# A seven-product form of the output matmul in a cross-attention and MoE kernel on Trainium2

## The chip, the core and the metric

The kernel runs on one core of one Trainium2 chip. A core has a matrix engine (TensorE, "PE" in the profile), a vector engine (VectorE, "DVE"), an activation engine (ScalarE, "ACT"), a general engine (GpSimd, "POOL") and a queue engine (SyncE, "SP") that here only issues DMAs. TensorE reads from the on-chip memory SBUF and writes to PSUM, eight accumulation banks of 128 x 512 fp32; the other engines carry data from there to SBUF. Each engine works through its own instructions in order; semaphores tie the engines together. The metric is the device time of one launch in microseconds (us), the median of several runs.

## What is computed

`x` is (8 batches, 8 heads, 512 tokens, 64), `state` is (8, 8, 32 slots, 64). Tokens attend to the slots and the slots to the tokens; both results are put side by side along the sequence and go through one feed-forward layer with 2048 hidden units.

```python
scores = scale * np.matmul(x, state.transpose(0, 1, 3, 2))   # softmax over slots -> a
xread = np.matmul(a, state)
scores2 = scale * np.matmul(state, x.transpose(0, 1, 3, 2))  # softmax over tokens -> a2
sread = np.matmul(a2, x)
y = np.concatenate([xread, sread], axis=2)     # then (B * 544, 512)
h = y @ w_in                                   # 512 -> 2048
g = h * (1.0 / (1.0 + np.exp(-h)))             # SILU
out = g @ w_out                                # 2048 -> 512
```

## The kernel before

Matmuls are in bf16 with fp32 sums, and the output is fp32. Nothing is left to a scheduler: the order in which the program is written is the order of each engine's queue.

The read of the tokens is folded into the first layer. For each batch `W1[b]` = state x w_in (256 slot rows x 2048) is made by small tiled matmuls (`w1_mms`, L470, eight matmuls of 32 output rows that share the array, called a piece of 512 columns) and carried to SBUF by `w1_out`, half on VectorE and half on ScalarE. The normalised weights `a`, transposed, are `aT[b]`. So h of a batch, hidden tile ft (16 tiles of 128), is two accumulating matmuls of 512 columns, `W1[b]` x `aT[b]`: `emit_G1(k)`, L525, k = 16 b + ft. It goes to one of the two PSUM buffers `h1` of the pool psH, and ScalarE's SILU (L554) writes it to SBUF as `gt[k]`, 128 hidden units x 512 tokens. `upto(k)` issues all of these up to k.

The output product, `G2(b, tt, ft)` (L563), takes 128 tokens (block tt of 4) of `gt`, all 512 output columns of `w_out_sb[:, ft]`, and sums over the 16 ft in one PSUM bank, tag o0 or o1 of psO. `store(b, tt, eng)` copies a finished bank to SBUF, with VectorE for blocks 0 and 3 and ScalarE for 1 and 2, and SP issues the DMA of 256 KB.

Batch 0 has a loop of its own (L658 to L723) that also makes the first W1. Batches 1 to 7 (L734 to L803) run through tt and ft, 64 matmuls of 512 columns each. Between them stand, at places written out as `at == (tt, ft)`:
- in block 0, the rest of the batch's own `emit_G1`, one before each G2, six ahead (three in batch 1); in block 3, the first six of the next batch;
- at (1, 4), or (1, 6) in batch 1: the scores for batch b + 2 (`scores_t`, in one bank of psO and one of psH), two W1 pieces (in the four banks a0 to a3 of psA, by `bank`), in batches 1, 4 and 6 the state rows' products (`sread`, L417, in psH), then their way out on VectorE and ScalarE;
- at (2, 8) of batches 1, 2, 4 and 5: two more W1 pieces in the banks and a third in psH;
- casts and transposes of x and the norm (`norm_t`) of batch b + 2 at (3, 0). ScalarE loads another function table before the exponentials and one after.

The state rows (256 of them) are the last, "batch 8": `place_xm` gathers them on VectorE in `xmT` (eight copies, at (0, 4) and (0, 8) of batch 7), their `emit_G1` (L543, four matmuls of 256 columns) stand in blocks 1 to 3 of batch 7, and their output is `G2(8, 0, ft)`, and `last_cols` (L585) for the other 128 rows.

Of the kernel before, what the change touches and what calls it, by code (L numbers as in the profile page):

```python
# [8 lines left out]
FP32 = mybir.dt.float32  # L9
# [33 lines left out]
def kernel(  # L43
# [13 lines left out]
    pers = ctx.enter_context(tc.tile_pool(name="pers", bufs=1))  # L57
    xpool = ctx.enter_context(tc.tile_pool(name="xpool", bufs=2))
    xtpool = ctx.enter_context(tc.tile_pool(name="xtpool", bufs=2))
    att = ctx.enter_context(tc.tile_pool(name="att", bufs=4))  # L60
    epool = ctx.enter_context(tc.tile_pool(name="epool", bufs=6))
    wpool = ctx.enter_context(tc.tile_pool(name="wpool", bufs=2))
    tpool = ctx.enter_context(tc.tile_pool(name="tpool", bufs=2))
    e2pool = ctx.enter_context(tc.tile_pool(name="e2pool", bufs=4))
    gpool = ctx.enter_context(tc.tile_pool(name="gpool", bufs=28))
    opool = ctx.enter_context(tc.tile_pool(name="opool", bufs=4))
    psO = ctx.enter_context(tc.tile_pool(name="psO", bufs=1, space=bass.MemoryType.PSUM))
    psH = ctx.enter_context(tc.tile_pool(name="psH", bufs=2, space=bass.MemoryType.PSUM))
    psA = ctx.enter_context(tc.tile_pool(name="psA", bufs=1, space=bass.MemoryType.PSUM))
# [16 lines left out]
    stT = pers.tile([128, B, 4, 2, NS], BF16)  # L86
    w_in_sb = pers.tile([128, 4, DF], BF16)
    w_out_sb = pers.tile([128, NFT, DM], BF16)
    xs = pers.tile([128, B, 128], BF16)
    xmT = pers.tile([128, 2, 4, NS, 4], BF16)  # L90
    x_rows = []
# [232 lines left out]
    eT = {}  # L324

    def scores_t(b):
        scT_ps[0] = psO.tile([128, 512], FP32, tag="o1", name="ps_scT")
        scT_ps[1] = psH.tile([128, 512], FP32, tag="h1", name="ps_scT")
        for s in range(4):
            for hg in range(2):  # L330
                h = HEAD_OF_SLOT[hg][s]
                r = 64 * (h % 2)
                nc.tensor.matmul(  # L333
                    scT_ps[hg][ds(32 * s, 32), :],
                    stT[ds(r, 64), b, h // 2, s % 2, :],
                    xT[b][ds(r, 64), :, h // 2, :],
                    start=True,
                    stop=True,
                    tile_position=(r, 32 * s),
                    skip_group_check=True,  # L340
                )
# [63 lines left out]


    def sread(bs):
        ps = psH.tile([128, 512], FP32, tag="h1", name="ps_sr")
        for i, b in enumerate(bs):
            to = ps[:, ds(132 * i, 132)]  # L410
            for hg in range(2):
                for c in range(4):
                    for s in range(4):
                        h = HEAD_OF_SLOT[hg][s]
                        odd = h % 2
                        at = PAD + XW * (4 * c + h // 2) + (64 if odd else -1)
                        nc.tensor.matmul(  # L417
                            to[ds(32 * s, 32), ds(66 * hg + odd, 65)],
                            exp_nat[b, hg][:, c, s, :],
                            x_rows[b % NX][:, ds(at, 65)],  # L420
                            start=(c == 0),
                            stop=(c == 3),
                            tile_position=(0, 32 * s),
                            skip_group_check=True,
                        )
        return ps
# [65 lines left out]

    h1 = {}
    gt = {}
    outs = {}

    h_ps = {}

    def g1_first():
        for k in range(2):  # L500
            gt[k] = gpool.tile([128, 512], BF16, tag="g", name="g")
        pss = [psH.tile([128, 512], FP32, tag="h1", name="h1") for _ in range(2)]
        ps1 = psA.tile([128, 512], FP32, tag="a1", name="h1")
        for i in range(2):
            for k, to in ((0, pss[i][:, 0:256]), (1, ps1[:, ds(256 * i, 256)])):
                for hg in range(2):
                    nc.tensor.matmul(  # L507
                        to,
                        W1[0][:, hg, ds(128 * k, 128)],
                        aT[0][:, hg, ds(2 * i, 2), :],  # L510
                        start=(hg == 0),
                        stop=(hg == 1),
                        skip_group_check=True,
                    )
        for i in range(2):
            nc.scalar.activation(
                gt[0][:, ds(256 * i, 256)], pss[i][:, 0:256], func=SILU, bias=0.0
            )
        nc.scalar.activation(gt[1][:], ps1[:], func=SILU, bias=0.0)

    def g1_half(k, hg):
        b, ft = divmod(k, NFT)
# [11 lines left out]
    def emit_G1(k):  # L534
# [14 lines left out]
                    skip_group_check=True,  # L549
                )  # L550
        n = 512 if b < B else 256
        g = gpool.tile([128, 512], BF16, tag="g", name="g")
        gt[k] = g
        nc.scalar.activation(g[:, 0:n], ps[:, 0:n], func=SILU, bias=0.0)  # L554

    def G2(b, tt, ft):
        if ft == 0:
            if b == 0 and tt >= 2:
                outs[tt] = psA.tile([128, DM], FP32, tag=f"a{tt - 2}", name="o_a")
            else:  # L560
                i = (tt + (b > 0)) % 2 if tt < 3 else 0
                outs[tt] = psO.tile([128, DM], FP32, tag=f"o{i}", name="o")
        nc.tensor.matmul(  # L563
            outs[tt][:],
# [4 lines left out]
            skip_group_check=True,  # L569
        )  # L570

    def store(b, tt, eng):
        o = opool.tile([128, DM], FP32, tag="o_sb", name="o_sb")
        copy(eng, o[:], outs[tt][:])
        if b < B:
            nc.sync.dma_start(out_re[ds(136 * b, 128), tt, :], o[:])
# [81 lines left out]
    for ft in range(12):  # L658
# [3 lines left out]
        if ft in W0:  # L662
# [4 lines left out]
            if ft in W1_AT:  # L667
                w1_out(1, [(W1_AT[ft], 512)], both, pss1)
            ready = sum(W0[ft]) // 128
        if ft == 11:  # L670
            for hg in range(2):
                cast_x(1, nc.vector, 0, 4, 4 * hg, 4)
# [54 lines left out]
    def w1_next(k, new=bank):  # L727
# [3 lines left out]
            done.append((i, cols, both, w1_mms(i, cols, new)))  # L731
        return done

    for b in range(1, B):  # L734
        n = b + 1
        m = n + 1
        lead = 3 if b == 1 else 6
        for tt in range(4):
            for ft in range(NFT):
                at = (tt, ft)  # L740
                if tt == 0:
                    upto(NFT * b + min(lead + ft, NFT))
                if b == B - 1 and at in ((0, 4), (0, 8)):
                    place_xm(at[1] // 8, nc.vector)
                if b == 1:
                    if at == (0, 1):
                        transpose_x(3)
                    if at == (0, 4):
                        for u in range(2):
                            evict_state(u, nc.vector)  # L750
                        spread_x(2)
                    if at == (0, NFT - lead):
                        for hg in range(2):
                            scores(2, hg)
                        for hg in range(2):
                            exps(2, hg)
                    if at == (1, 0):
                        for hg in range(2):
                            norm(2, hg, (((nc.gpsimd, nc.vector)[hg], 0, 4),))
                            transpose_a(2, hg)  # L760
                elif at == (0, NFT - lead) and m < B:
                    nc.scalar.activation(warm[:], busy[:, 0:1], func=EXP, bias=0.0)
                if m + 1 < B:
                    if at == (0, 2):
                        for h in range(0, H, 4 if b < 3 else H):
                            load_x(m + 1, h, 4 if b < 3 else H, nc.sync)
                    if at == (1, 0):
                        for c in range(4):
                            cast_x(m + 1, nc.gpsimd, c, 1)
                    if at == (2, 10):  # L770
                        transpose_x(m + 1)
                if n < B and at == (1, 6 if b == 1 else 4):
                    if m < B:
                        scores_t(m)
                    pss = w1_next(2)
                    srs = SREAD_AT.get(b, ())
                    if srs:
                        ps_sr = sread(srs)
                    if m < B:
                        exps_t(m)  # L780
                        nc.scalar.activation(warm[:], busy[:, 0:1], func=SILU, bias=0.0)  # L781
                    w1_out(*pss[0])
                    if srs:
                        sread_out(srs, ps_sr)
                    w1_out(*pss[1])
                if m < B:
                    if at == (2, 0):
                        spread_x(m)
                    if at == (3, 0):
                        norm_t(m)  # L790
                if n < B:
                    if at == (2, 8) and b in (1, 2, 4, 5):
                        pss = w1_next(2) + w1_next(1, new_h)
                        for i in (2, 0, 1):
                            w1_out(*pss[i])
                    if tt == 3 and ft % 2 == 1 and ft // 2 < 6:
                        upto(NFT * n + ft // 2 + 1)
                elif tt > 0 and (ft % 3 == 2 or ft == NFT - 1):
                    upto(min(done[0] + 1, NFT * (B + 1)))
                G2(b, tt, ft)  # L800
            store(b, tt, nc.scalar if tt in (1, 2) else nc.vector)
        for ft in range(NFT):
            gt.pop(NFT * b + ft)  # L803
    for ft in range(NFT):
        upto(NFT * B + ft + 2)
        G2(B, 0, ft)
# [32 lines left out]
```

## Time and profile before

| | |
|---|---|
| timed runs | 212.98 us median (212.7, 212.98, 213.41) |
| profiled execution, its span | 306.5 us |
| mean granted TensorE clock in it | 0.661 of full speed |
| output matmuls L563 to psO, 512 columns | 496, busy 189.3 us |
| first-layer matmuls L525, 512 columns | 252, busy 104.3 us |
| SILUs of 512 columns, ScalarE | 126, mean 597 ns |
| output copies, VectorE and ScalarE | 15 at 691 ns, 16 at 597 ns |
| x casts on GpSimd | 24, mean 648 ns |
| output stores, SP | 33 DMAs of 256 KB (median), 2.4 us to landing |

The profiled execution took longer than the timed runs, and the profile shows with which clock its matrix engine ran; a reading must say which of the two it speaks of. "Busy" is the union of an engine's instructions, "mean" the recorded duration of one; matmuls overlap, so that their mean is longer than their spacing. A group's last entry is the time the engine stood idle before it, and what ended most of that.

### The profile page before, as it was taken

How to read it: one execution, taken by the hardware profiler on the slowest of the kernel's cores; microseconds unless marked ns; L12 is line 12 of the kernel's file. 1: busy time of each engine (PE TensorE's matmuls, PEld its weight loads, DVE VectorE, ACT ScalarE, POOL GpSimd, SP SyncE). 2: the span in 40 equal slices, each digit the busy share in tenths (PEclk: the TensorE clock that was granted, in tenths of full speed). 3: DMA queues.
4: the chain of work that ended last, by engine and by line, in shares of the span. 5: the costliest groups of instructions: out<-in, count | busy, mean ns of one | idle time of the engine just before them, and what ended most of it. 6: DMA issues, size and time to landing. Idle time of an engine off the chain costs nothing.

```text
span 306.5 us, 3871 instructions
## 1 busy us (share of the span) xinstructions
PE 301.5 (98%) x1576; PEld 120.1 (39%) x1576; DVE 73.9 (24%) x146; ACT 141.0 (46%) x244; POOL 40.1 (13%) x62
## 2 busy tenths in 40 slices
PE   8999999999999999999999999999999999999995
PEld 3433443343333333333333333333333333355544
DVE  4521347244400350032001350035002104000000
ACT  4744556674546533672446453664353044322310
POOL 8640143022202010111002010000100000000000
PEclk9666666666666666666666666666666666666666
DMA  8999438715722251515251261020200100000102
GB/s 196 200 206 273 141 130 222 225 34 81 175 90 81 72 137 34 171 49 124 68 171 37 50 157 49 0 71 37 66 34 36 43 34 36 0 34 34 36 34 68
DMA packets 42978, 28.65 MB, mean 93 GB/s; under 512 B 27601, under 2 KB 37841, under 8 KB 42961
## 3 DMA queue, kind: packets, MB, share of 16 engines
q1 hardware_dynamic: 36752, 20.65, 24.3%
q0 software_dynamic: 5920, 7.64, 12.2%
q8 instruction: 12, 0.20, 0.3%
q10 hardware_dynamic: 288, 0.13, 0.1%
q14 instruction: 6, 0.04, 0.0%
HBM read 17.43 MB, written 8.91 MB: 86 GB/s over the span
## 4 chain that ended last, share of the span: by engine, by line
PE 98%; ACT 1%; DVE 0%; issue 0%
PE o L563 53%; PE h L525 27%; PE ps_w L470 4%; PE h L543 3%; PE o_a L563 3%; PE ps_busy L165 2%; PE o_part L585 2%; PE ps_sr L417 1%; PE ps_xt L254 1%; PE ps_scT L333 1%; PE ps_sc L307 1%; PE ps_at L399 0%; ACT xT L157 0%; PE h L507 0%; ACT exp_nat L321 0%
## 5 line engine op out<-in xcount | busy, mean ns | idle before, releaser
L563 PE MATMUL o<-w_out_sb,g 128*128 128x512 bf16 x496 | 189.3, 512 | 0.0
L554 ACT ACTIVATE g<-h 128x512 bf16<-128x512 f32 (+1 forms) x142 | 81.4, 573 | 92.4 <-PE h L525 73.1
L525 PE MATMUL h<-aT,W 128*128 128x512 bf16 x252 | 104.3, 514 | 0.0
L563 PEld LDWEIGHTS <-g 128*128 128x128 bf16 x528 | 62.5, 121 | 100.5 <-issue 96.7
L525 PEld LDWEIGHTS <-W 128*128 128x128 bf16 x252 | 30.2, 121 | 51.5 <-issue 50.3
L159 DVE COPY o_sb<-o 128x512 f32<-128x512 f32 x15 | 10.4, 691 | 157.9 <-PE o L563 148.0
L159 DVE CAST W<-ps_w 128x512 bf16<-128x512 f32 (+1 forms) x35 | 22.0, 669 | 43.2 <-PE ps_w L470 43.2
L157 ACT ACTIVATE W<-ps_w 128x512 bf16<-128x512 f32 (+1 forms) x31 | 16.1, 579 | 19.3 <-PE ps_w L470 19.3
L157 ACT ACTIVATE o_sb<-o 128x512 f32<-128x512 f32 x16 | 9.5, 597 | 32.3 <-PE o L563 28.4
L159 POOL CAST x_nat<-x_f 128x512 bf16<-128x512 f32 x24 | 14.6, 648 | 46.8 <-issue 33.0
L363 POOL TENSOR_TENSOR an<-e,rcn 128x512 bf16<-128x512 bf16 x5 | 7.6, 1517 | 83.3 <-DVE rcn L361 83.3
L563 PE MATMUL o_a<-w_out_sb,g 128*128 128x512 bf16 x32 | 13.9, 510 | 0.0
L543 PE MATMUL h<-xmT,w_in_sb 128*128 128x256 bf16 x64 | 13.4, 349 | 0.0
L470 PE MATMUL ps_w<-w_in_sb,stT 64*32 64x512 bf16 (+1 forms) x264 | 13.0, 483 | 0.0
L543 PEld LDWEIGHTS <-w_in_sb 128*128 128x128 bf16 x64 | 7.6, 119 | 7.7 <-issue 6.2
L347 ACT ACTIVATE eT<-ps_scT 128x512 bf16<-128x512 f32 x10 | 5.4, 595 | 7.2 <-PE ps_scT L333 7.2
L165 PE MATMUL ps_busy<-busy 128*128 128x512 bf16 x15 | 6.4, 575 | 1.2 <-DVE warm L172 1.2
L383 POOL TENSOR_TENSOR an<-exp_nat,rc 128x512 bf16<-128x512 bf16 x3 | 3.1, 1047 | 26.1 <-DVE rc L381 26.1
L360 DVE TENSOR_REDUCE rs<-e 128x32 f32<-128x1024 bf16 x5 | 6.1, 1211 | 1.9 <-DMA e<-eT 1.9
L781 ACT ACT_TABLE_LOAD x5 | 6.4, 1283 | 0.1
L470 PEld LDWEIGHTS <-stT 64*32 64x32 bf16 x264 | 3.3, 94 | 7.4 <-issue 6.8
L109 POOL DMA_DIRECT2D x_f<-in_x_dram x4 | 3.3, 831 | 17.0 <-DVE x_rows L159 14.4
(76 smaller groups left out, 112.1 us busy)
## 6 DMA issues: line engine op xcount, KB each, us to landing
out_dram<-o_sb SPq DMA_DIRECT2D x33, 256.0 KB, 2.4
x_f<-in_x_dram SPq DMA_DIRECT2D x6, 512.0 KB, 4.6
x_f<-in_x_dram POOLq DMA_DIRECT2D x2, 1024.0 KB, 10.2
x_f<-in_x_dram SPq DMA_DIRECT2D x2, 1024.0 KB, 6.2
w_out_sb<-in_moe_w_out_dram POOLq DMA_DIRECT2D x6, 256.0 KB, 10.3
w_in_sb<-in_moe_w_in_dram POOLq DMA_DIRECT2D x3, 512.0 KB, 9.8
x_f<-in_x_dram POOLq DMA_DIRECT2D x2, 512.0 KB, 14.3
w_in_sb<-in_moe_w_in_dram POOLq DMA_DIRECT2D x2, 256.0 KB, 6.6
```

The source lines that it names most:

```text
L157: nc.scalar.activation(dst, src, func=COPY, bias=0.0)
L159: eng.tensor_copy(dst, src)
L165: nc.tensor.matmul(ps[:], busy[:, 0:128], busy[:], start=True, stop=True, skip_group_check=True)
L360: nc.vector.tensor_reduce(rs[:], e2[b][:], axis=AX, op=ADD)
L363: eng.tensor_tensor(a[:, hg], e2[b][:, hg], rc[:, hg].to_broadcast([128, 4, 4, NS]), op=MULT)
L470: nc.tensor.matmul(pss[f, hg][ds(32 * s, 32), 0:n], stT[ds(r, 64), b, h // 2, s % 2, :], w_in_sb[ds(r, 64), h // 2, ds(f, n)], start=True, ...
L525: nc.tensor.matmul(h_ps[k][:], W1[b][:, hg, ds(128 * ft, 128)], aT[b][:, hg, :, :], start=(hg == 0), stop=(hg == 1), skip_group_check=True,)
L543: nc.tensor.matmul(ps[:, 0:256], w_in_sb[:, kt, ds(128 * ft, 128)], xmT[:, :, kt].rearrange("p t n b -> p t (n b)"), start=(kt == 0), stop ...
L554: nc.scalar.activation(g[:, 0:n], ps[:, 0:n], func=SILU, bias=0.0)
L563: nc.tensor.matmul(outs[tt][:], gt[b * NFT + ft][:, ds(128 * tt, 128)], w_out_sb[:, ft, :], start=(ft == 0), stop=(ft == NFT - 1), skip_gr ...
L585: nc.tensor.matmul(ps[:, 0:n], gt[b * NFT + ft][:, ds(128 * tt, 128)], w_out_sb[:, ft, cols], start=(ft == 0), stop=(ft == NFT - 1), skip_ ...
L781: nc.scalar.activation(warm[:], busy[:, 0:1], func=SILU, bias=0.0)
```

## The change

For batches 1 to 7 the product g (512 tokens x 2048) times w_out (2048 x 512) is cut in two in each direction: tokens 0 to 255 and 256 to 511, hidden tiles 0 to 7 ("lo") and 8 to 15 ("hi"), output columns 0 to 255 and 256 to 511 (blocks B11, B12, B21, B22 of w_out). Instead of eight half products, seven are made, with sums of blocks as operands. Four sums of weight blocks (`wt`, D1 to D4) are made once, in batches 0 and 1 (`t_weights`). In each batch VectorE makes S1 = lo2 + hi2 and S2 = S1 - lo1 (`sums12`), then hi1 - S2 in place (`sums4`) and lo1 - lo2 in place (`sums3`), where 1 and 2 are the token halves.

Each product has 8 steps k of two matmuls of 256 columns (`Unit.mm`). Products 1, 6, 5 and 7 run on in one bank `al`; after 1, 6 and 5 its state is copied to SBUF (`snap`, on VectorE, ScalarE, ScalarE). Products 2, 4 and 3 each have the other bank, `be`. The four output blocks come from these by three adds out of `be` on VectorE, a subtraction and an addition on GpSimd, and a copy on ScalarE. They gather in two SBUF tiles of 256 tokens, and SP stores each with one DMA. The last block of a batch is finished in the next one (`finish_last`).

Order in a batch: its remaining `emit_G1` with products 1 and 2 among them (13 of 16 steps by a pacing rule); the rest of 2; scores, W1 pieces (`PIECES_A`) and sread (in batch 1 behind product 6); product 6; 4; 5; W1 pieces (`PIECES_B`); 3 and 7, with the next batch's first six `emit_G1`. `norm_t` for batch b + 1 stands in batch b (before, for b + 2). Both banks of scores_t are now in psH, and sread takes a bank of psA. `gt` lies in three tiles of eight hidden tiles each; fewer buffers in two other pools pay for the new tiles.

```diff
-    att = ctx.enter_context(tc.tile_pool(name="att", bufs=4))
+    att = ctx.enter_context(tc.tile_pool(name="att", bufs=2))
...
-    gpool = ctx.enter_context(tc.tile_pool(name="gpool", bufs=28))
-    opool = ctx.enter_context(tc.tile_pool(name="opool", bufs=4))
+    gpool = ctx.enter_context(tc.tile_pool(name="gpool", bufs=3))
+    opool = ctx.enter_context(tc.tile_pool(name="opool", bufs=1))
+    o1pool = ctx.enter_context(tc.tile_pool(name="o1pool", bufs=3))
+    spool = ctx.enter_context(tc.tile_pool(name="spool", bufs=1))
...
     def scores_t(b):
-        scT_ps[0] = psO.tile([128, 512], FP32, tag="o1", name="ps_scT")
-        scT_ps[1] = psH.tile([128, 512], FP32, tag="h1", name="ps_scT")
+        for hg in range(2):
+            scT_ps[hg] = psH.tile([128, 512], FP32, tag="h1", name="ps_scT")
...
     def sread(bs):
-        ps = psH.tile([128, 512], FP32, tag="h1", name="ps_sr")
+        ps = bank([128, 512], FP32, "ps_sr")
...
+        def snap(self, eng):
+            t = spool.tile([128, 2, 256], FP32, tag=f"snap{len(self.kept) % 2}", name="snap")
+            self.kept.append(t)
+            copy(eng, t[:], self.al[:])
...
+        def mm(self, p, k):
+            hi, lo = self.hi, self.lo
+            left, right = {
+                1: (lambda: lo[:, k, 0:256], B11),
+                2: (lambda: hi[:, k, 0:256], B21),
+                3: (lambda: hi[:, k, 0:256], B22),
+                4: (lambda: hi[:, k, 256:512], D4),
+                5: (lambda: self.s1[:, k], D1),
+                6: (lambda: self.s2[:, k], D2),
+                7: (lambda: lo[:, k, 256:512], D3),
+            }[p]
...
+            for t in range(2):
+                nc.tensor.matmul(
+                    to[:, t, :],
+                    left[:, ds(128 * t, 128)],
+                    right[:, k, :],
+                    start=first and t == 0,
+                    stop=(k == 7),
+                    skip_group_check=True,
+                )
...
+        def sums12(self, k0, n):
+            k = ds(k0, n)
+            add(nc.vector, self.s1[:, k], self.lo[:, k, 256:512], self.hi[:, k, 256:512])
+            sub(nc.vector, self.s2[:, k], self.s1[:, k], self.lo[:, k, 0:256])
...
+    PIECES_A = {1: 1, 2: 2, 3: 2, 4: 1, 5: 2, 6: 2}
+    PIECES_B = {1: 3, 2: 3, 3: 3, 4: 3, 6: 2}
...
+    def finish_last(u):
+        copy(nc.scalar, u.block(1, 1), u.al[:])
+        add(nc.gpsimd, u.block(1, 0), u.block(1, 0), u.block(1, 1))
+        u.out_half(1)
...
+            if j == lead + 1:
+                if prev is not None:
+                    finish_last(prev)
...
+            early(j)
+            if j == 13:
+                u.sums12(0, 4)
+                if b == 1:
+                    t_weights((4,), 4, 4)
+        u.sums12(4, 2)
+        while todo:
+            u.mm(*todo.pop(0))
+        u.sums12(6, 2)
+        add(nc.vector, u.block(0, 0), u.be[:], u.kept[0][:])
...
+        for k in range(8):
+            u.mm(6, k)
+            if n == B and k in (2, 5):
+                place_xm(k // 3, nc.vector)
...
+        u.snap(nc.scalar)
...
+        u.sums4()
...
+        for k in range(8):
+            u.mm(4, k)
+            sread_g1(step)
+            step += 1
+        add(nc.vector, u.block(1, 0), u.be[:], u.kept[1][:])
...
+        u.sums3()
+        for k in range(8):
+            u.mm(5, k)
...
+        u.snap(nc.scalar)
+        sub(nc.gpsimd, u.block(1, 0), u.block(1, 0), u.kept[2][:])
+        if b in PIECES_B:
+            c = PIECES_B[b]
+            pss = w1_next(2) + (w1_next(1, new_h) if c == 3 else [])
+            for i in (2, 0, 1)[3 - c :]:
+                w1_out(*pss[i])
+        for p in (3, 7):
+            for k in range(8):
+                u.mm(p, k)
...
+                if n < B and i % 2 == 1 and i // 2 < LEADS:
+                    upto(NFT * n + i // 2 + 1)
+            if p == 3:
+                add(nc.vector, u.block(0, 1), u.be[:], u.kept[2][:])
+                u.out_half(0)
```

## The prediction

> **What bounds the kernel now.** I read the page first, then the windows by stage, then the groups with shapes kept apart, then the timeline at a few places. From the page:
>
> ```profile
> span 306.5 us, 3871 instructions
> ...
> PE 301.5 (98%) x1576; PEld 120.1 (39%) x1576; DVE 73.9 (24%) x146; ACT 141.0 (46%) x244; POOL 40.1 (13%) x62
> ...
> PEclk9666666666666666666666666666666666666666
> ...
> PE 98%; ACT 1%; DVE 0%; issue 0%
> ```
>
> TensorE is busy 98% of the span, and the chain that ended last is TensorE for 98%: fewer matmul columns is the right thing to want. But the clock row says that this execution ran at about 0.65 of full clock after the first slice. The windows give the scale:
>
> ```profile
> core 0: us, PE busy (x) PEld busy (x) DVE busy (x) ACT busy (x) POOL busy (x), PEclk, DMA share, GB/s
> 0.00:17.00 17.00, 15.10 (x96) 7.07 (x96) 8.61 (x27) 10.06 (x20) 12.96 (x24) 0.78 1.07 199
> ...
> sum 306.00, PE 301.45 PEld 120.13 DVE 73.89 ACT 140.99 POOL 40.09; mean PE 33.49 PEld 13.35 DVE 8.21 ACT 15.67 POOL 4.45
> ```
>
> After 17 us TensorE is busy 301.45 - 15.10 = 286.35 us and idle 289.5 - 286.35, about 3 us. At full clock the busy part would be 286.35 x 0.65 = 186 us, so the span 17 + 186 + 3 = 206 us. The runs have 212.98; the other 7 us are what lies around the span and waits that a slow clock hides. So the timed runs go at full clock. I therefore price TensorE's work at 0.65 of its traced duration and every other engine's at the traced duration, and make the sum against 212.98. In the profile's own state (306.5 us) the same saving is larger and the same waits shorter.
>
> **The price of a column.**
>
> ```profile
> 101.30 0.91 PE L470 MATMUL ps_w<-w_in_sb,stT 64*32 64x512 bf16 x16
> 102.13 6.64 PE L563 MATMUL o<-w_out_sb,g 128*128 128x512 bf16 x20
> ...
> 297.94 5.41 PE L585 MATMUL o_part<-w_out_sb,g 128*128 128x256 bf16 x48
> ```
>
> Twenty 512-column matmuls take 6.64 us; without the last one's 0.52 us this is 0.322 us each, 0.63 ns a column. The 48 of L585 are 16 of 256 columns and 32 of 128, 8192 columns; without the last (0.27 us) 5.14 us for 8064, 0.64 ns. Narrow matmuls, each with its own weight load, pay no visible extra. At full clock a column is 0.63 x 0.65 = 0.41 ns.
>
> Removed per batch 1 to 7: 64 matmuls of 512 columns, 32,768. Added: 7 products x 8 x 2 = 112 of 256 columns, 28,672. Saved 4,096 a batch, 28,672 in all: **11.8 us** (18 us at the profile's clock). Below I write G for one feed-forward tile (two matmuls of 512, 0.42 us) and U for one product step (two of 256, 0.21 us).
>
> What could take this away is the weight load, of which there are 112 instead of 64:
>
> ```profile
> L563 PEld LDWEIGHTS <-g 128*128 128x128 bf16 x528 | 62.5, 121 | 100.5 <-issue 96.7 <-ACT g L554 1.4 <-ACT g L516 0.3
> L585 PE MATMUL o_part<-w_out_sb,g 128*128 128x128 bf16 x32 | 2.8, 265 | 0.0
> ```
>
> One load is recorded with 121 ns, more than the 105 ns of a 256-column matmul at full clock. If loads could not overlap, 112 x 121 ns = 13.6 us a batch would eat the gain. But L585 issues a 128-column matmul with its load every 2.8 / 32 = 88 ns, so the 121 ns overlap. [...]
>
> **What VectorE gets.** Per batch 8,192 bf16 elements in sums (each operand bf16 in SBUF), three adds out of PSUM and one snapshot; it loses two output copies. ScalarE gets two snapshots and a copy for two copies; GpSimd two fp32 adds. No row has a bf16 sum of this kind. The rows around it:
>
> ```profile
> L360 DVE TENSOR_REDUCE rs<-e 128x32 f32<-128x1024 bf16 x5 | 6.1, 1211 | 1.9 <-DMA e<-eT 1.9
> L159 DVE COPY x_rows<-x_nat 128x2048 bf16<-128x2048 bf16 x6 | 4.1, 685 | 0.0
> L363 DVE TENSOR_TENSOR an<-e,rcn 128x512 bf16<-128x512 bf16 x5 | 3.5, 691 | 0.2
> L383 DVE TENSOR_TENSOR an<-exp_nat,rc 128x512 bf16<-128x512 bf16 x3 | 2.8, 922 | 0.1
> L159 DVE CAST W<-ps_w 128x512 bf16<-128x512 f32 x33 | 21.3, 685 | 43.2 <-PE ps_w L470 43.2
> L159 DVE COPY xT<-ps_xt 128x1024 bf16<-128x1024 bf16 x2 | 1.4, 692 | 3.3 <-PE ps_xt L254 3.3
> L159 DVE COPY xmT<-xs 64x256 bf16<-64x256 bf16 x8 | 3.0, 372 | 0.1
> ```
>
> 1024 bf16 elements cost between about 0.4 us (the 2048-element copy's rate) and 1.21 us (the reduce). I take 0.69, the PSUM copy of 1024, and 0.43 for 512. Back to back an instruction of 0.69 costs 0.60 (four W casts took 2.48 us).
>
> ```profile
> 48.17 2.48 DVE L159 CAST W<-ps_w 128x512 bf16<-128x512 f32 x4
> ...
> 54.92 0.81 PE L525 MATMUL h<-aT,W 128*128 128x512 bf16 x2
> 55.57 0.52 PE L563 MATMUL o<-w_out_sb,g 128*128 128x512 bf16 x1
> 55.77 0.60 ACT L554 ACTIVATE g<-h 128x512 bf16<-128x512 f32 x1 [0.34 <-PE h L525]
> ```
>
> A SILU starts 0.20 us after TensorE is free of its G (55.77 against 55.57) and takes 0.60; a waiting TensorE takes some 0.05 more. Let E be the end of a batch's last G.
>
> **The waits that come in.** Before, five output matmuls of token block 0 (and whole blocks after it) lie between a batch's last G and the first use of its SILU; now three U.
> - *Last step of product 2.* It reads the last SILU, ready at E + 0.85; TensorE has three U, 0.63, before it. 0.2 x 7 = 1.5 us.
> - *Copy of the previous batch's last block* on ScalarE between two SILUs. G has two PSUM buffers; ten G and 13 U take 6.9 us against ten SILUs at 0.6. The copy mostly fits: 0.1 x 6 = 0.6 (0 to 0.6 each).
> - *Third W1 piece in the G buffers,* now two U before the next batch's first G instead of nine matmuls: 0.20 + 0.69 + 0.05 against 0.42 and the burst's tail, 0.4 wait in batches 2 to 4: 1.2.
> - *Batch 6:* two W1 pieces take all four banks, and sread, moved from the G buffers to these banks, needs the first back. VectorE empties it behind sums (E + 0.80 to 1.70), the first add (2.35), the two sums for product 3 (3.55) and the cast (4.25). TensorE is there at E + 1.06 + 0.6: 2.6 us.
> - *Batch 7:* the state rows' eight xmT copies (3.0 us) stand on VectorE behind the same sums and add, so end at E + 5.35. The first G for them follows one U after product 6, E + 2.95: 2.4 us. Before, they stood at ft 4 and 8 of the first token block, a dozen output matmuls ahead of it.
> - *Batch 1:* VectorE has three late weight sums, the norm (2.8), two sums, a cast, sread_out (1.4) in line: about 8.2 from E + 1.2, so E + 9.3. TensorE needs the sread bank for its W1 pieces at E + 8.6 (0.7 wait), and then the third piece's bank after one add, two sums and a cast, E + 11.9, against E + 10.4: 2.2 in all.
> - *One more tiled burst* (batch 3): 0.15. The four weight sums of batch 0 (3.3 us) fill VectorE's idle 6.3 us before 34.14 at the slow clock, 4 at full: nothing. Without that cover, at 1.21 per 1024, about 2.
>
> Stores on SP are two of 512 KB for four of 256 KB; out halves, aT transposes and x loads queue behind GpSimd's add early in the batch, but their readers come over 6 us later: nothing. Waits: 1.5 + 0.6 + 1.2 + 2.6 + 2.4 + 2.2 + 0.15 = 10.6 us. Sum: 212.98 - 11.8 + 10.6 = **211.8 us**.
>
> **Rivals.**
> 1. *The waits hide* (chance 0.18). Sums at the fast end (0.4), and TensorE runs ahead where I let it wait: half of 10.6 gone, 206.5 us. For it: VectorE 24% and ScalarE 46% busy. Against: the waits are chains of order on one queue, not load.
> 2. *VectorE meets GpSimd* (0.33, slower). L383's multiply, alone 0.69 us as in L363, has a mean of 0.92 beside GpSimd. A sum that waits out one x cast (0.6 us on GpSimd) delays the third W1 piece: two sums x 0.6 in four batches, 4.8, and some 2 in batch 1: 218.5 us. It decides from about 0.2 us a batch on, since only 1.2 us are left over. [...]
> 3. *Sums at one element a cycle* (0.04): 1.21 for 0.69, some 4 us more VectorE a batch, at least 2.5 of it on TensorE: 229 us.
> 4. *Nothing to measure* (0.12): waits of 11.2 to 12.4 cancel the saving. The measurement can't tell 0.3% (0.64 us) from none.
> 5. *The narrow matmuls save nothing* (0.01): 213 + 10 = 223.
>
> My forecast, a small gain of about 1 us (209 to 212.3), has 0.32.
>
> **How the numbers follow.** Faster by over 0.3%: 0.32 + 0.18 = 0.50. Within: 0.12. Slower: 0.33 + 0.04 + 0.01 = 0.38. The forecast is 211.8. The likeliest case's own range is 209 to 212.3; with the two large rivals the range goes to 205 (saving whole, two fifths of the waits) and 220 (rival 2 and a little more), leaving the two dear rivals out.
>
> **What would show it.** Columns: the product line's 256-column matmuls at about 0.63 ns a column if the clock is 0.65 again. Sums: 1024 bf16 at 0.6 to 0.7 us; at 1.2 rival 3 holds. Waits: TensorE released by VectorE in front of sread in batch 6, of the state rows' first G in batch 7, and late in batch 1; in a 0.65 execution shorter than here. Sums that stretch to 1 us beside GpSimd's casts show rival 2. TensorE busy without gaps, at 98%, would show rival 1, and then my order of queues is wrong.

## The result and the profile after

The changed kernel takes 214.61 us (median of seven runs, 213.44 to 216.66) against 212.76 us (212.66 to 213.41) for the kernel before on the same chip: ratio 1.0082, 95% interval [1.0056, 1.0107]. It is slower by a little less than one per cent; the forecast was 211.8 us and a small gain.

The page of the changed kernel, its head, the clock row and the chain that ended last:

```profile
span 214.9 us, 4628 instructions
...
PE 200.9 (94%) x1893; PEld 131.5 (61%) x1912; DVE 126.8 (59%) x237; ACT 141.1 (66%) x251; POOL 58.3 (27%) x76
...
PEclk9999999999999999999999999999997999999999
...
PE 78%; DVE 13%; DMA 4%; ACT 2%; issue 2%; SPq 0%; DVEq 0%
```

Behind its start this execution ran at full clock but for one slice, so its microseconds can be compared with the timed runs. TensorE has fallen from 98% of the chain to 78% (the kernel before at full clock, further below, has 91%), and VectorE has come up to 13%: the change has put VectorE in line with TensorE. Of the profiled run's 216.66 us, 1.8 us lie around the span. The record of the granted clock begins, at full, at 13.84 us; in the profile of the kernel before it begins at 6.4. (The row shows 9 where the record has no entry; up to 12.1 us TensorE's filling matmuls of 512 columns start 427 ns apart, and later matmuls of 512 columns 216.) The late start makes up about 2 us of the span, an estimate: the profile of its twin with copies (further below), which starts like this one (21 and 20 matmuls from 9 to 12 us), takes 214.8 - 188.26 = 26.5 us up to tile 10 of batch 0, that of the kernel before with copies (34 matmuls there) 211.5 - 187.07 = 24.4. This execution lies 2.05 us over the median.

What TensorE waits for, by the profile's list of waits (total us, times, longest):

```profile
PE ps_sr L420 <- DVE W L162: 2.4, 1, 2.4
PE h L558 <- DVE xmT L162: 1.8, 2, 1.4
...
PE h L540 <- DVE W L162: 1.1, 1, 1.1
PE ps_w L473 <- DVE xm L441: 0.9, 1, 0.9
PE h L540 <- ACT W L160: 0.8, 4, 0.2
```

The names are those of the forecast's terms: sread's bank in batch 6, the xmT copies in batch 7, batch 1 (two lines), the third W1 piece. The list counts idle time only; from the start of one matmul to the start of the next, less the usual spacing, they lose 2.5, 2.1, 1.2, 1.05 and 1.4 us (0.37 in each of three batches, 0.33 in batch 1). The last step of product 2 shows as a wait of its weight load, seven times:

```profile
PEld L648 <- ACT g L568: 2.2, 7, 0.3
```

It costs 0.2 us a batch. The copy of the last block on ScalarE is too small for the list, but it is paid as well. In each of batches 2 to 7 one G1 tile starts 0.09 us late, 0.5 us in all, because the SILU that frees its bank stands behind the copy:

```profile
69.40 0.59 ACT L160 ACTIVATE o_sb<-o 128x512 f32<-128x512 f32 x1
69.58 0.59 PE L540 MATMUL h<-aT,W 128*128 128x512 bf16 x2
69.88 1.09 ACT L568 ACTIVATE g<-h 128x512 bf16<-128x512 f32 x2
70.01 0.60 PE L648 MATMUL o<-w_out_sb,g 128*128 128x256 bf16 x4
...
70.53 0.38 PE L540 MATMUL h<-aT,W 128*128 128x512 bf16 x1
```

The largest wait is read best in the timeline of batch 6 (start, duration, engine, line, operation; what ended the idle time in brackets):

```profile
161.22 0.63 PE L473 MATMUL ps_w<-w_in_sb,stT 64*32 64x512 bf16 x16
...
162.28 1.28 DVE L591 TENSOR_TENSOR g<-g,s 128x1024 bf16<-128x1024 bf16 x2
163.48 0.68 DVE L162 CAST W<-ps_w 128x512 bf16<-128x512 f32 x1
164.21 1.07 PE L420 MATMUL ps_sr<-x_rows,e 128*32 128x65 bf16 x64 [2.37 <-DVE W L162]
165.22 2.99 PE L648 MATMUL o<-wt,s 128*128 128x256 bf16 x16
...
168.04 1.91 PE L648 MATMUL o<-wt,g 128*128 128x256 bf16 x16
```

VectorE does the two sums for product 3 first and only then the cast that frees the bank; TensorE starts sread 0.05 us after the cast has ended. What follows was in no term of the forecast: the sixteen matmuls of product 6 take 2.99 us, the same sixteen of product 4 take 1.91. The windows around it (start and end, length, busy us of PE, PEld, DVE, ACT and POOL, then the granted clock, the DMA share and GB/s) show the clock:

```profile
160.60:164.00 3.40, 1.21 (x21) 0.35 (x19) 3.09 (x6) 0.24 (x1) 0.00 (x0) 1.00 0.01 1
164.00:167.40 3.40, 3.19 (x75) 2.47 (x75) 1.90 (x7) 0.00 (x0) 0.00 (x0) 0.50 0.02 5
...
187.90:191.30 3.40, 1.63 (x14) 1.16 (x13) 3.26 (x9) 0.82 (x2) 0.00 (x0) 1.00 0.00 0
```

In the 3.4 us in which TensorE idled it was busy for 1.21 us, and for the next 3.4 us its clock was granted at half. In batch 7, behind a stretch with 1.63 us busy, it stayed at full. Six of the seven timed runs of the changed kernel have a mean clock of 0.992, which is one such stretch; the seventh has 1.000 and is the fastest (213.44 us).

### The profile page after: what moved, and what is told of

It reads as the page before. It is cut to its first block, busy times and chain, and to the rows that moved or that the text cites. A ratio compares the mean times of both kernels' runs of the same rounds, so it can differ in the third digit from the quotient of the medians.

```text
span 214.9 us, 4628 instructions
## 1 busy us (share of the span) xinstructions
PE 200.9 (94%) x1893; PEld 131.5 (61%) x1912; DVE 126.8 (59%) x237; ACT 141.1 (66%) x251; POOL 58.3 (27%) x76
## 4 chain that ended last, share of the span: by engine, by line
PE 78%; DVE 13%; DMA 4%; ACT 2%; issue 2%; SPq 0%; DVEq 0%
PE o L648 36%; PE h L540 21%; PE o L577 5%; PE ps_w L473 3%; PE h L558 3%; PE o_a L577 3%; DMA x_f<-in_x_dram 2%; DVE g L591 2%; DMA st_x<-st_b 2%; PE o_part L691 2%; DVE xmT L162 1%; PE ps_xt L257 1%; DVE o_sb L594 1%; DVE stT L162 1%; DVE W L162 1%
## 5 line engine op out<-in xcount | busy, mean ns | idle before, releaser
L540 PE MATMUL h<-aT,W 128*128 128x512 bf16 x237 | 70.6, 379 | 1.9 <-DVE W L162 1.1
L648 PE MATMUL o<-w_out_sb,g 128*128 128x256 bf16 x336 | 54.4, 273 | 0.9
L540 PEld LDWEIGHTS <-W 128*128 128x128 bf16 x252 | 24.4, 98 | 10.3 <-issue 3.5
L648 PE MATMUL o<-wt,g 128*128 128x256 bf16 x224 | 29.9, 273 | 0.0
L594 DVE TENSOR_TENSOR o_sb<-o,snap 128x512 f32<-128x512 f32 x21 | 14.4, 688 | 24.8 <-PE o L648 22.7
L648 PE MATMUL o<-wt,s 128*128 128x256 bf16 x224 | 28.5, 280 | 0.0
L648 PEld LDWEIGHTS <-s 128*128 128x128 bf16 x224 | 22.0, 100 | 4.3 <-DVE s L591 1.3
L591 POOL TENSOR_TENSOR o_sb<-o_sb,snap 128x512 f32<-128x512 f32 x7 | 9.2, 1311 | 44.8 <-ACT snap L160 40.4
L577 PE MATMUL o<-w_out_sb,g 128*128 128x512 bf16 x46 | 12.9, 380 | 0.1
L594 DVE TENSOR_TENSOR s<-g 128x512 bf16<-128x512 bf16 (+1 forms) x21 | 10.7, 508 | 2.1 <-ACT g L568 2.1
L591 DVE TENSOR_TENSOR g<-g 128x1024 bf16<-128x1024 bf16 x14 | 11.5, 865 | 0.0
## 6 DMA issues: line engine op xcount, KB each, us to landing
w_out_sb<-in_moe_w_out_dram POOLq DMA_DIRECT2D x6, 256.0 KB, 10.5
```

What stands on the lines that cost most here:

```text
L540: nc.tensor.matmul(h_ps[k][:], W1[b][:, hg, ds(128 * ft, 128)], aT[b][:, hg, :, :], start=(hg == 0), stop=(hg == 1), skip_group_check=True,)
L577: nc.tensor.matmul(outs[tt][:], gt[b * NFT + ft][:, ds(128 * tt, 128)], w_out_sb[:, ft, :], start=(ft == 0), stop=(ft == NFT - 1), skip_gr ...
L591: eng.tensor_tensor(dst, a, c, op=SUB)
L594: eng.tensor_tensor(dst, a, c, op=ADD)
L648: nc.tensor.matmul(to[:, t, :], left[:, ds(128 * t, 128)], right[:, k, :], start=first and t == 0, stop=(k == 7), skip_group_check=True,)
```

## The experiments

In all of these kernels the six transfers that transpose on the way (of x, of the states, of the exponentials, twice of the normalised weights, of the state read) are plain copies of the same bytes on the same queue. They leave the transposition out, so their output is not the reference's, and only their times and traces count here. The first two runs say what this does to the time. The kernel before was timed again beside each group of runs, at 212.75 or 212.76 us. Each edit was made on top of the copies:

```diff
-        nc.sync.dma_start_transpose(
-            t.rearrange("q c k p -> q (c k) p"),
+        nc.sync.dma_start(
+            t.rearrange("q c k p -> q (c k p)"),
             x_nat[b].rearrange("p c k w -> p (c k w)"),
```

### The pair: before and after, with copies

> The kernel before, with each of its transfers that transpose on the way (of x, of the states, of the exponentials, of the normalised scores, of the state read) made a plain copy of the same bytes on the same queue, so its output is not the reference's. It serves as the base of its twin after the change, and shows for the first time where the kernel before waits at a full clock. Theory W (the change saves 11.3 us of output columns and gives them back in waits listed in the trace after, 9.8 us, and in a stretch at half clock): TensorE has no wait over 0.3 us behind batch 0, time 212.8 us within 1 us, because the transfers were not on its path. Rival S (the kernel before waits too, and the change removed less than columns times pitch, or the copies were on the path): over 1.5 us of TensorE waits behind batch 0, or a time over 1 us away from 212.8.

Measured: 212.70 us (212.63 to 213.29, 10 runs), ratio to the kernel before 0.9996 [0.9983, 1.0009]. The transfers are not on the path of the kernel before, and its profile is now at full clock:

```profile
span 211.5 us, 3871 instructions
...
PE 205.9 (97%) x1576; PEld 97.3 (46%) x1576; DVE 73.7 (35%) x146; ACT 139.3 (66%) x244; POOL 39.7 (19%) x62
...
PE 91%; DMA 5%; DVE 1%; POOL 0%; ACT 0%; issue 0%; POOLq 0%
```

TensorE's list of waits has four entries, all in the first stage or in batch 0: 1.2 us once for the first filling matmul, 0.4 for a load of w_in, 0.3 and 0.2 for `xT`. Behind batch 0 there is none. Rival S falls: the kernel before gives nothing back. Nine output matmuls in a row give the price of a column:

```profile
56.32 2.12 PE L563 MATMUL o<-w_out_sb,g 128*128 128x512 bf16 x9
```

By their starts they are 216 ns apart, the 256-column ones after the change 109 ns (16 in 1.91 us, the last of them 0.27). 256 columns more thus cost 107 ns, 2.4 columns a nanosecond, and some 2 ns are left over for each matmul. So the change saves 7 x (64 x 216 - 112 x 109) ns = 11.3 us.

> The changed kernel with the same transfers made plain copies, so its output is not the reference's. Theory W: 214.6 us within 1 us, 1.9 us more than its twin before the change (1.0 to 2.8), with the same TensorE waits as in the trace after: 2.5 us in batch 6, 2.1 in batch 7, about 2.7 in batch 1, 0.37 three times at the third W1 piece, 0.2 seven times. Rival T (the transposing transfers themselves cost the changed kernel its 1.9 us): the difference to the twin falls under 0.5 us.

Measured: 214.26 us (212.25 to 216.61, 10 runs), ratio 1.0041 [1.0013, 1.0068], 1.6 us over its twin (1.3 without its two longest runs, 215.92 and 216.61 us, which leave a median of 214.04). The waits are there at much the same size (2.50 in batch 6, 1.52 and 0.57 in batch 7). Rival T falls. The ten runs sort themselves by clock: the two with a mean of 1.000 take 212.25 and 212.46 us, less than the twin; the eight with 0.992 take 213.65 to 216.61.

### The clock

```diff
+            if b == 6:
+                keep_busy(11, psH, "h1")
             ps_sr = sread(srs) if srs else None
```

> The changed kernel with copies, and with eleven idle 512-column products on zeros put on TensorE in batch 6 just before the state read, so that it works through its 2.4 us wait; nothing else differs, the wait itself stays as long. Theory W (the wait makes the clock be granted at half for 3.4 us, which costs 1.2 to 1.7 us more than the wait): 1.2 to 1.7 us faster than the changed kernel with copies, and the stretch 165 to 169 us at clock 1.0. Rival H (the half clock is there whatever TensorE does, or costs nothing): same within 0.3 us or slower.

Measured: 212.91 us (212.23 to 214.15, 10 runs), 1.35 us less than without the filling (1.1 without those two longest runs) and the same as the kernel before (1.0017 [0.9996, 1.0038]). sread starts as long after the W1 piece as without it (3.0 us), so nothing was shortened; only the clock stayed up (a mean of 0.998 or more in all ten runs). From the start of sread in batch 6 to the end of the span the profiles have 50.70 us without the filling and 49.21 with it: the half clock costs **1.5 us**. From the first matmul of batch 0's tile 10 on, where the start of the kernel no longer enters, they have 188.26 and 186.41 us; the other 0.36 of this difference lies ahead of the wait, most of it in batch 1. So at full clock the changed kernel takes 186.4 to 186.8 us from there on, 0.3 to 0.7 less than the 187.07 of the kernel before.

> The changed kernel with copies, and three idle 512-column products on zeros, not eleven, ahead of the state read in batch 6: TensorE still idles 1.8 us or so of its 2.4. In batch 7 of every trace 2.1 us of waits within some 2.4 us leave the clock at full. Theory W2 (what counts is how much of one 3.41 us stretch of the clock's record is idle, and the limit lies between 2.1 and 2.5 us): no half clock in any run, time as with eleven, 212.9 us within 0.7. Rival K (any idle of that order lowers it, and batch 7 is spared by the place of its stretch): the clock falls as in the changed kernel with copies, 214.3 us, mean clock 0.992 in most runs.

Measured: 213.06 us (212.28 to 213.59, 10 runs), ratio 1.0003 [0.9986, 1.0019], a mean clock of 0.998 or more in every run. Three products that need 0.65 us are enough:

```profile
160.40:163.80 3.40, 1.78 (x75) 1.62 (x75) 2.51 (x8) 0.00 (x0) 0.00 (x0) 1.00 0.03 5
163.80:167.20 3.40, 3.40 (x33) 3.05 (x32) 1.48 (x3) 1.58 (x3) 0.00 (x0) 1.00 0.09 19
```

Behind the wait of 1.6 us no run had the half clock; behind the wait of 2.4 us, without the products, eight runs of ten had it. Rival K falls. The clock is recorded in stretches of 3.41 us. In the changed kernel's profile the stretch with the wait of batch 6 leaves 2.22 us idle, and the one with the two waits of batch 7 leaves 1.77; the wait shortened by three products is 1.62 us in all. Two runs further below give one more value each, behind their last matmuls. With 1.26 us busy, 2.15 idle (the run with the casts later), the next stretch was granted half, with 1.45 busy, 1.96 idle (the run with the copies early), full clock:

```profile
201.27:204.68 3.41, 1.26 (x23) 1.09 (x20) 0.58 (x2) 0.00 (x0) 0.00 (x0) 1.00 0.36 120
204.68:206.06 1.38, 0.00 (x0) 0.00 (x0) 0.00 (x0) 0.00 (x0) 0.00 (x0) 0.50 0.00 0
```

```profile
202.68:206.09 3.41, 1.45 (x27) 1.28 (x23) 0.58 (x2) 0.09 (x1) 0.00 (x0) 1.00 0.41 141
206.10:207.60 1.50, 0.00 (x0) 0.00 (x0) 0.00 (x0) 0.00 (x0) 0.00 (x0) 1.00 0.00 0
```

### The waits of batches 6 and 7

```diff
-    PIECES_A = {1: 1, 2: 2, 3: 2, 4: 1, 5: 2, 6: 2}
-    PIECES_B = {1: 3, 2: 3, 3: 3, 4: 3, 6: 2}
+    PIECES_A = {1: 1, 2: 2, 3: 2, 4: 1, 5: 2, 6: 1}
+    PIECES_B = {1: 3, 2: 3, 3: 3, 4: 3, 6: 3}
```

> The changed kernel with copies, and in batch 6 one W1 piece behind the first state read and three at the second place, instead of two and two: the state read's bank is then not one that a W1 cast of VectorE still has to empty. Theory W: the 2.4 us wait goes, and the half clock behind it, against 0.4 us of one more third piece: 3.2 us faster than the changed kernel with copies (2.4 to 4.0). Rival B (the wait moves to the second place, where three pieces need six banks): under 1 us faster.

Measured: 210.92 us (210.42 to 212.01, 4 runs), 3.34 us less than the changed kernel with copies (3.1 without its two longest runs), 0.9918 [0.9885, 0.995] of the kernel before. One W1 piece leaves two banks free, and in batch 6 sread follows at once:

```profile
158.90 0.41 PE L473 MATMUL ps_w<-w_in_sb,stT 64*32 64x512 bf16 x8
159.24 0.69 PE L420 MATMUL ps_sr<-x_rows,e 128*32 128x65 bf16 x64
159.87 1.92 PE L648 MATMUL o<-wt,s 128*128 128x256 bf16 x16
```

The wait and the half clock behind it are gone, and batch 6 has the 0.37 us of a third piece that the expectation charged.

```diff
         for j in range(lead, NFT):
             upto(NFT * b + j + 1)
+            if n == B and j in (8, 9):
+                place_xm(j - 8, nc.vector)
...
         for k in range(8):
             u.mm(6, k)
-            if n == B and k in (2, 5):
-                place_xm(k // 3, nc.vector)
```

> As the run with the W1 piece of batch 6 moved (210.92 us), and VectorE's eight copies of xmT in batch 7 are issued during the first products instead of in the sixth. Theory W: the two waits on xmT in batch 7 (1.52 and 0.57 us) go, 2.1 us less: 208.8 us (208.2 to 209.4). Rival M (they only move: VectorE's snapshot and sums come late behind 3.07 us of copies, and TensorE waits for those): over 210.0 us.

Measured: 208.76 us (208.54 to 209.43, 4 runs), 2.16 us less than with the piece moved alone. The copies are the same; they only no longer stand behind sums in VectorE's line. Rival M falls.

### VectorE beside GpSimd

```diff
-        if m + 1 < B:
-            for c in range(4):
-                cast_x(m + 1, nc.gpsimd, c, 1)
...
-        if m + 1 < B:
-            transpose_x(m + 1)
         u.sums3()
...
                 w1_out(*pss[i])
+        if m + 1 < B:
+            for c in range(4):
+                cast_x(m + 1, nc.gpsimd, c, 1)
+            transpose_x(m + 1)
```

> As the run before it, and GpSimd's four casts of x for the batch after next, and their transfer, stand behind the W1 casts instead of beside the sums for products 4 and 7; the work is the same. Theory W (contention makes the VectorE sums longer, up to 1.98 us for two instead of 1.28, but hardly reaches TensorE): within 0.5 us of the run before it. Rival V (VectorE late beside GpSimd is what eats the gain): at least 1.0 us faster than the run before it.

Measured: 207.88 us (207.37 to 209.84, 4 runs), 0.9 us less: between the two theories. The trace says where. In batch 1, without the move, first, then with it:

```profile
57.56 0.62 PE L473 MATMUL ps_w<-w_in_sb,stT 64*32 64x512 bf16 x15 [0.90 <-DVE xm L441]
58.02 2.36 DVE L591 TENSOR_TENSOR g<-g 128x1024 bf16<-128x1024 bf16 x2
...
58.25 1.58 POOL L591 TENSOR_TENSOR o_sb<-o_sb,snap 128x512 f32<-128x512 f32 x1 [4.40 <-DVE o_sb L594]
...
61.03 0.38 PE L540 MATMUL h<-aT,W 128*128 128x512 bf16 x1 [1.08 <-DVE W L162]
```

```profile
55.31 1.27 PE L473 MATMUL ps_w<-w_in_sb,stT 64*32 64x512 bf16 x24
```

The W1 pieces of batch 1 no longer wait (1.05 us), nor does a step of product 6 (0.46 us in that profile). From batch 2 to batch 3 (last step of product 2 to last step of product 2) the two take 21.55 and 21.54 us. Beside each other both are longer: without the move the casts' mean is 684 ns and that of the sums for product 7 is 798, with it 651 and 760. In the changed kernel the two sums of a batch that stand beside the casts take 1.90, 1.70 and 1.74 us (batches 2 to 4), those of batch 5, beside no GpSimd work, 1.28. But the sums beside the casts reach TensorE in batch 1 alone, and cost about 1 us there. GpSimd's subtraction was not moved. The two sums beside it take 2.36 us in both runs, the subtraction 1.58, and the third W1 piece, whose cast stands behind them on VectorE, makes TensorE wait 1.08 us in both (the last line of the first view). So up to another 1.1 us of batch 1's waits may lie in this pair; no run tried that. The longer durations show which instructions grow, not whether anybody waits for them.

### The order of issue

```diff
-            t_weights((3,), 4, 4)
             for hg in range(2):
                 scores(2, hg)
...
-        u.sums3()
...
-        u.snap(nc.scalar)
-        sub(nc.gpsimd, u.block(1, 0), u.block(1, 0), u.kept[2][:])
...
-            pss = w1_next(2) + (w1_next(1, new_h) if c == 3 else [])
-            for i in (2, 0, 1)[3 - c :]:
-                w1_out(*pss[i])
+            if c == 3:
+                pss = w1_next(1, new_h)
+            pss = pss + w1_next(2)
+            if c == 3:
+                w1_out(*pss.pop(0))
+        u.snap(nc.scalar)
+        sub(nc.gpsimd, u.block(1, 0), u.block(1, 0), u.kept[2][:])
+        for piece in pss:
+            w1_out(*piece)
+        if b == 1:
+            t_weights((3,), 4, 4)
+        u.sums3()
```

> As the first run of this call, and three places in the order of issue differ: the third W1 piece is multiplied first of the three and cast ahead of ScalarE's snapshot; the sums for product 7 and the last part of D3 stand behind VectorE's W casts. Theory W: the 0.37 us waits of batches 2, 3, 4 and 6 go (1.5 us), and in batch 1 those of 1.05, 0.33 and 1.24 us (2.6), together 4.1 us: 204.7 us (204.0 to 206.0). Rival M (the sums then come late for product 7, or the casts' banks): less than 2 us faster than the first run.

This edit stands on the run with the copies early (208.76 us, in the expectation "the first run"), without the later casts. Measured: 205.44 us (204.92 to 206.22, 4 runs), 3.3 us less instead of 4.1. In batch 1 one wait of about 0.2 us is left, for VectorE's add, and the 0.37 us of the third piece turn into 0.16, for the first SILU that now stands behind the snapshot on ScalarE. Rival M falls.

```diff
-                and (n_todo - len(todo)) * (NFT - lead) < 13 * (j + 1 - lead)
+                and (n_todo - len(todo)) * (NFT - lead) < 11 * (j + 1 - lead)
```

> As the run before it, and fewer steps of products 1 and 2 are put between the G1 tiles (factor 11 instead of 13), so that five steps instead of three are left behind the last G1. Theory W: the 0.2 us wait of product 2's last step for ScalarE goes in each of seven batches, 1.4 us less: 203.3 us (202.5 to 204.5). Rival A (ScalarE cannot keep the faster pace of the G1 tiles, and TensorE waits for their banks instead): same within 0.5 us, or slower.

Measured: 205.63 us (204.75 to 206.09, 4 runs), no difference to 205.44: Rival A holds. The waits at product 2's end are gone, but in the batches with a block left over from the batch before another has come in:

```profile
86.59 0.59 ACT L160 ACTIVATE o_sb<-o 128x512 f32<-128x512 f32 x1
87.20 0.38 PE L648 MATMUL o<-w_out_sb,g 128*128 128x256 bf16 x2
87.72 0.59 PE L540 MATMUL h<-aT,W 128*128 128x512 bf16 x2
```

With fewer steps between the tiles, the copy that ScalarE makes in `finish_last` between two SILUs delays the next bank of the G1 tiles by 0.31 us (TensorE is through at 87.42), six times in all. At the old pace the same copy costs 0.09 us each time, so 1.3 us are lost here for the 1.4 gained. (This profile also has a wait of 0.8 us for a sum at product 6 of batch 1, which comes and goes between the profiles.) To cover the wait without touching the pace, on top of the new order (205.44 us) again:

```diff
         while todo:
+            if len(todo) == 1:
+                u.mm(6, 0)
+                u.mm(6, 1)
             u.mm(*todo.pop(0))
...
-        for k in range(8):
+        for k in range(2, 8):
             u.mm(6, k)
```

> As the run with three places in the order of issue changed (205.44 us), and two steps of product 6 stand ahead of the last step of product 2, whose operand ScalarE is still making. Theory W: they cover its 0.2 us wait in all seven batches without slowing the G1 tiles, 1.4 us less: 204.0 us (203.3 to 204.8), 4.1% under the kernel before. Rival M (the wait moves to the next transfer of a bank, as with the slower pace): same within 0.5 us.

Measured: 203.95 us (203.67 to 205.16, 5 runs), ratio to the kernel before **0.9589 [0.9561, 0.9617]**, 1.5 us less than 205.44: Theory W holds, and rival M falls. It holds the edits of batches 6 and 7 and the order above. Its page has TensorE back at the share it had before, in a shorter span:

```profile
span 202.6 us, 4646 instructions
...
PE 195.7 (97%) x1912; PEld 129.6 (64%) x1912; DVE 126.6 (62%) x237; ACT 140.2 (69%) x251; POOL 55.7 (28%) x76
```

This version beats both kernels, with copies in place of the transposing transfers; with those it was not run.

## Why the prediction was wrong

| term | forecast us | measured us |
|---|---|---|
| columns saved | -11.8 | -11.3 |
| last step of product 2 | 1.5 | 1.4 |
| copy of the last block on ScalarE | 0.6 | 0.5 |
| third W1 piece | 1.2 | 1.1 |
| batch 6, sread's bank | 2.6 | 2.5 |
| batch 7, xmT | 2.4 | 2.1 |
| batch 1 | 2.2 | 2.6 |
| half clock behind batch 6 | none | 1.5 |
| burst and everything else | 0.15 | about 0.8 |

"Measured" is from the traces at full clock. The last row is what is left over: from tile 10 of batch 0 on, the changed kernel with copies takes 188.26 us and its twin 187.07, 1.2 more; -11.3, the waits (10.2) and 1.5 make 0.4. Of the remainder 0.38 us lie behind the last matmul (3.75 us from its start to the span's end instead of 3.37), and a part at changes between full and tiled matmuls (in batch 2 the first tiled one behind product 5 starts 0.20 us after the last full one, not 0.11); the rest was not followed.

The waits were the forecast's good half: 10.5 without the burst against 10.2 us, each at the place named. In batch 1 the agreement is partly luck: the forecast's 2.2 us came from the order of the queue alone, while about 1 us of the 2.6 went when the casts on GpSimd were moved. The step that failed is the sentence "So the timed runs go at full clock. I therefore price TensorE's work at 0.65 of its traced duration". It priced a wait at its own length and took the clock as given, while behind the longest wait of the change, 2.4 us, the clock was 0.50 for 3.4 us, and with that idle time filled, wholly or in part (the two fill runs), it was not. With the clock kept up the changed kernel ties with the one before, which was the forecast's rival 4; the half clock and its 1.5 us make it slower. Two sizes were off besides: the saving by 0.5 us (0.41 ns a column, from a slow profile, against 216 ns for 512 and 109 for 256), and the remainder. The 7 us that the forecast called "what lies around the span and waits that a slow clock hides" were no waits either: 1.8 us lie around the span, and behind batch 0 TensorE does not wait. The rest is the scale. A 512-column matmul took 322 ns in the slow profile and takes 216 at full clock, a factor of 0.67 and not 0.65; 286.35 us times 0.67 are 192 us, and the span comes to 212, as the profile of the kernel before at full clock has it (211.5).

The rivals. 1, the waits hide: refuted, all were paid. 2, VectorE meets GpSimd, the forecast's slower case: the sums beside GpSimd are longer (two take 1.70 to 1.90 us beside the casts and 2.36 beside the subtraction, 1.28 beside nothing), but the price named, 6.7 us, is not there. It assumes sums that wait out a whole cast, 0.6 us each; no run shows that, and in the changed kernel's profile a sum beside the casts is longer by 0.4 us at most (1.10 instead of 0.68). Moving the casts gave 0.9 us, in batch 1, and the subtraction may hold up to 1.1 more there; in the other batches the third piece is released by ScalarE (the list of waits says "ACT W"). So the time did become longer, as rival 2 had it, but what the forecast's sum lacked was the half clock; the 0.9 us in batch 1 lie within a term that the sum had. 3, slow sums: refuted, 1024 elements take 0.68 us and 512 take 0.42, as the forecast took them. 5, narrow matmuls that save nothing: 109 ns with a weight load each, refuted.

Open: why the clock came up as late as 13.84 us in the profiled run of the changed kernel (and, to judge by its 21 matmuls from 9 to 12 us, as late in that of its twin with copies; the kernel before with copies has 34 there), where the first stage is the same text in all kernels. No run tried a cause.

## What to carry to other kernels

Where TensorE sets the end, a saving in matmuls is an advance that the queues of the other engines must be re-ordered to keep: here the same seven products are 0.8% slower than eight in the order they came in, and 4.1% faster after six moves in the order of issue, with no arithmetic removed (and with plain copies for the transposing transfers). Look first at what stands ahead of the instruction that frees a PSUM bank. And count the idle time of TensorE not only by its length: here a wait of 2.4 us was worth filling with products on zeros (1.35 us), though it could not be shortened by that.

## What the runs showed of the hardware

- The granted clock is recorded in stretches of 3.41 us: in the changed kernel's profile the entries last 150.19, 3.413 and 47.79 us, which are 44, 1 and 14 times that. Half clock came behind stretches in which TensorE was idle for 2.15 us (the run with the casts later) and 2.22 (the changed kernel), full clock behind stretches with 1.77 (the changed kernel) and 1.96 (the run with the copies early). The record begins 13.84 us into the span of the changed kernel and 6.4 us into that of the kernel before. Why the same wait was followed by half clock in eight runs of ten and not in the other two was not shown; those two left no trace.
- The profiled run of the kernel before stood at 0.65 from 6.4 us on; the later ones have means of 0.992 to 1.000. Its durations times 0.65 are not those at full clock: 322 ns become 209, and 216 were measured.
- Plain copies for transposing transfers changed the time of the kernel before by 0.06 us, and that of the changed kernel by 0.35 (214.61 and 214.26 us).
